# Forward attention: exponentials over three PSUM banks in two slots, and a new TensorE order for it

## The chip, the cores and the metric

The kernel runs on one core of a Trainium2 chip. The metric is the device time of one execution in microseconds. Before the change its median over three runs is 2441.95 us (2440.43 to 2444.49). The engines are TensorE (PE in the profile; PEld is its weight load), VectorE (DVE), ScalarE (ACT), GpSimd (POOL) and SyncE (SP, which here only issues DMAs).

## The reference

One transformer block (2048 tokens, width 512, 32 heads of 16, a dense layer of 1792 with a squared ReLU, modulated layer norms) is computed forward, and then the gradients of all of its inputs but one. What the change touches is the softmax of the forward attention:

```
scores = jnp.einsum('bhqd,bhkd->bhqk', q, k) * Dh ** (-0.5)
p = _softmax(scores, axis=-1)
o = jnp.einsum('bhqk,bhkd->bhqd', p, v)
```

With 32 heads and 2048 x 2048 scores for each, 134 million exponentials have to be taken forward (and once more in the gradient, which the change leaves alone).

## The kernel before

After a short preparation the forward attention runs as 512 *units* (`funits`, NF = 512): 4 chunks of 512 queries, by 8 groups of 4 heads, by 16 tiles of 128 keys. One unit is one key tile of one head group for one query chunk: four heads, each a 128 x 512 block of scores, so four PSUM banks.

For a unit, `fscore` (L611) makes four score products. Each contracts over 32 rows (16 of the head, and one that carries a bound that is subtracted before the exponential), and the four heads use the four row groups of the TensorE array. They go in pairs: two products fill a two-bank tile `psST`, and one ACTIVATE (L622) takes the exponential of both banks, 128 x 1024, into the SBUF tile `ET`. `psST` has three slots (`bufs=3`, L1226), six of the eight PSUM banks.

`fpv` (L624) multiplies a unit's exponentials with the values: four products side by side in four column groups, added into `oacc`, one bank, over the 16 key tiles of a head group. After the 16th, VectorE copies `oacc` out (`ostage`, L640) before the next group may begin; the first unit of a group is called `begins` in the loop, and its `fpv` stands later in the order for that reason.

The eighth bank is `pm` (`mm()`, L157, a pool with one slot). It serves everything else that TensorE does meanwhile: the projections of the later heads in the first quarter, and then, for every query chunk that is finished, the dense layer forward and backward and the weight gradients. This work is cut into steps, one for a unit (`step`, `next_chain`, `next_ds`, and a table `plan` for the first 128 units). Most steps are one product of four matmuls into `pm` that VectorE then copies out (dsT L330, part L255, rz L458 and others); some products are spread over four units (L484, L538) and are read out only after the last. A unit without such a step gets two small filler matmuls (`steady`, L665). Which step belongs to which unit is counted in units, not in time.

The order of the instructions on every engine is the order in which the Python code makes them. TensorE takes them strictly in that order. For unit u it is: the scores of u; the value product of u - 2 (after the step, where that begins a head group); the step; filler. TensorE waits in three kinds of places: a score product waits until the exponential that last read its slot is done, a step waits until VectorE has emptied `pm`, and a value product waits for its exponentials.

Of the kernel before, what the change touches and what calls it, by code (L numbers as in the profile page):

```python
# [14 lines left out]
AF = mybir.ActivationFunctionType  # L15
ALU = mybir.AluOpType
AX = mybir.AxisListType
BF = dt.bfloat16
F32 = dt.float32

P = 128
# [7 lines left out]
SCALE = 0.25  # L29
# [5 lines left out]
def kernel(  # L35
# [8 lines left out]
    TT = n // P  # L44
# [8 lines left out]
    PE = nc.tensor  # L53
    DVE = nc.vector
    ACT = nc.scalar
# [89 lines left out]
    with ExitStack() as ph:  # L145
# [4 lines left out]
        ework = att.enter_context(tc.tile_pool(name="phCe", bufs=4, reuse_waits="tile"))  # L150
        b2row = ffw.tile([1, D], BF, name="b2row")
        racc = ffw.tile([P, 5, D], F32, name="racc")
        pools = {}
# [3 lines left out]
        def mm():  # L157
            products[0] += 1
            return pools["mm"].tile([P, 512], F32, name="pm", tag="pm")
# [21 lines left out]
        def later(lag, f, *args):  # L181
            due.append((unit[0] + lag, f, args, True))
# [4 lines left out]
        def run_due(everything=False):  # L187
            i = 0
            while i < len(due):
                if due[i][0] <= unit[0] or (everything and due[i][3]):  # L190
                    _, f, args, _ = due.pop(i)
                    f(*args)
                else:
                    i += 1
# [400 lines left out]
        funits = [(qc, hg, kt) for qc in range(QC) for hg in range(HG) for kt in range(TT)]  # L595
        fh, fe, fcur, fdone, dense = {}, {}, {}, [], []
# [4 lines left out]
        def fload(qc, hg):  # L601
            i = hg % 2
            kt_sb, qt_sb = kts[i], qts[i]
            rows = list(row_loads(kt_sb, qkT_st[1], hg, slice(0, n)))
            rows += row_loads(qt_sb, qkT_st[0], hg, slice(512 * qc, 512 * qc + 512), m_st)
            for i, (to, fro) in enumerate(rows):
                later(i // (2 if qc == 0 else 1), row_load, to, fro)
            run_due()
            fh[qc, hg] = (qt_sb, kt_sb)

        def fscore(u):  # L611
            qc, hg, kt = funits[u]
            qt_sb, kt_sb = fh[qc, hg]
            ET = ework.tile([P, 4, 512], BF, name="ET", tag="ET")
            fe[u] = ET
            for pair in range(2):
                ps = pools["s"].tile([P, 2, 512], F32, name="psST", tag="psST")
                for hi in range(2):
                    r = 32 * (2 * pair + hi)
                    PE.matmul(ps[:, hi, :], kt_sb[r:r + 32, kt * P:(kt + 1) * P], qt_sb[r:r + 32, :],  # L620
                              start=True, stop=True, tile_position=(r, 0))
                ACT.activation(ET[:, 2 * pair:2 * pair + 2, :], ps[:], AF.Exp, scale=SCALE)  # L622

        def fpv(u):  # L624
            qc, hg, kt = funits[u]
            if kt == 0:
                fcur["o"] = pools["o"].tile([P, 512], F32, name="oacc", tag="oacc")
                if hg == 0:
                    fcur["rr"] = ework.tile([H, 512], F32, name="rrows", tag="rrows", bufs=1)
                    fcur["ou"] = ework.tile([P, 4, HG, P], BF, name="O_un", tag="O_un", bufs=1)  # L630
            oacc = fcur["o"]
            ET = fe.pop(u)
            for hq in range(4):
                h = hg * 4 + hq
                lhsT = vaug[:, kt].rearrange("p h c -> p (h c)")[:, h * (DH + 1):h * (DH + 1) + 32]
                PE.matmul(oacc[32 * hq:32 * hq + 32, :], lhsT, ET[:, hq, :],  # L636
                          start=(kt == 0), stop=(kt == TT - 1), tile_position=(0, 32 * hq), skip_group_check=True)
            if kt == TT - 1:
                ostage = ework.tile([P, 512], F32, name="ostage", tag="ostage", bufs=1)
                DVE.tensor_copy(ostage[:], oacc[:])  # L640
                obf = ework.tile([P, 512], BF, name="obf", tag="obf", bufs=2)
                if u == NF - 1:
                    fcur["last"] = ostage
                    return
                if hg == HG - 1:
                    DVE.tensor_copy(obf[:], ostage[:])
                else:
                    POOL.tensor_copy(obf[:], ostage[:])
                for hq in range(4):
                    h = hg * 4 + hq  # L650
                    later(2, sp, fcur["rr"][h:h + 1, :], ostage[32 * hq + 16:32 * hq + 17, :])
                later(3, sp, fcur["ou"][:, :, hg, :], obf[:], True)
                if hg == HG - 1:
                    fdone.append((u + 7, qc, fcur["rr"], fcur["ou"]))

        def steady(u):
            if 0 <= u < NF and funits[u][2] == TT - 1:
                if dense or dwq or plan:
                    return
                pz = mm()  # L660
                for _ in range(2):
                    PE.matmul(pz[:], ones_bf[:], identb.unsqueeze(1).to_broadcast([P, 4, P]), start=True, stop=True)
            elif 0 <= u < NF:
                for _ in range(2):
                    PE.matmul(fcur["o"][0:DH, :], zeros[:], identb.unsqueeze(1).to_broadcast([P, 4, P]), start=False, stop=False,  # L665
                              tile_position=(0, 0), skip_group_check=True)
# [503 lines left out]
        NF = len(funits)  # L1170
# [44 lines left out]
        def early(u):  # L1215
            return u >= NF - 7 and "L" in loads and "O" not in loads["L"]
# [6 lines left out]
        plan_tasks()  # L1223
        stages = [*range(4, 14), *range(4), None, None, *range(14, 25)]
        with ExitStack() as ph2:
            pools["s"] = ph2.enter_context(tc.tile_pool(name="psS", bufs=3, space=bass.MemoryType.PSUM, reuse_waits="tile"))  # L1226
            pools["o"] = ph2.enter_context(tc.tile_pool(name="psO", bufs=1, space=bass.MemoryType.PSUM, reuse_waits="tile"))
            pools["mm"] = ph2.enter_context(tc.tile_pool(name="psM", bufs=1, space=bass.MemoryType.PSUM, reuse_waits="tile"))
            with tc.manual_schedule(engines={PE.engine, ACT.engine, DVE.engine, SP.engine, POOL.engine}):
                fh[0, 0] = (qts[0], kts[0])  # L1230
                for u in range(NF + 2):
                    unit[0] = u
                    run_due()
                    if u < NF:
                        if funits[u][2] == (10 if u < 7 * TT else 2) and u + TT < NF:
                            fload(*funits[u + TT][0:2])
                        fscore(u)
                    begins = TT <= u - 2 < NF and funits[u - 2][2] == 0
                    if 2 <= u and not begins:
                        fpv(u - 2)  # L1240
                    if u % 4 == 2 and u // 4 < len(stages) and stages[u // 4] is not None:
                        later_stage(stages[u // 4])
                    if u % 4 == 0 and 18 <= u // 4 < 32:
                        turn_weights(u // 4 - 18)
                    count, begun_group = products[0], open_group[0]
                    for f, args in plan.pop(u, ()):
                        f(*args)
                    if not dense and fqueue and fdone and u - 2 >= fdone[0][0]:
                        fqueue.pop(0)
                        qc, rr, ou = fdone.pop(0)[1:]  # L1250
                        ffinish(qc, rr, ou, chunk_loads(qc))
                    elif u < NF - 4 and not early(u):
                        step(u)
                    elif dwq and u >= NF - 2:
                        next_chain()
                    if begins:
                        fpv(u - 2)
                    if u in post:
                        post.pop(u)()
                    if products[0] == count and not (begun_group or open_group[0]):  # L1260
                        steady(u - 2)
                    if early(u):
                        early_finish()
                    if u == NF:
                        tiny = wk.tile([P, 1], F32, name="tiny", tag="tiny", bufs=1)
                        ACT.activation(tiny[:], onesf[:, 0:1], AF.Sqrt)
                while dense:
                    unit[0] += 1
                    run_due()
                    step(unit[0])  # L1270
# [381 lines left out]
    with ExitStack() as ph:  # L1652
        ework = ph.enter_context(tc.tile_pool(name="phIe", bufs=4, reuse_waits="tile"))
# [197 lines left out]
        if True:  # L1851
# [4 lines left out]
            for b in range(NU // 4):  # L1856
                toks, bank = order_t if on_pe(b - 1) else order_n
                for tok in toks:
                    c, i = tok[0], int(tok[1:] or 0)
# [409 lines left out]
```

## Time and profile before

| | |
|---|---|
| median of three runs | 2441.95 us |
| the profiled execution, and its span | 2435.86 us, 2434.1 us |
| first exponential of the forward attention starts, last ends | 37.1 us, 976.7 us |
| busy from 37.1 to 976.7 (939.6 us) | ACT 939.33, PE 872.11, DVE 485.68, POOL 303.62 us |
| the rest of the kernel after that (backward attention and the last gradients) | some 1457 us |

In a row of the costliest groups stand line, engine, operation, what is written and read, the shapes, the count, then the busy time in us and the mean ns of one, then the time that the engine stood idle just before them and what ended it. In a timeline row stand the start and the length in us, the engine and the line, and in brackets idle time before it. A mean of ACT's instructions is longer than their spacing, because an ACTIVATE is recorded from its dispatch, and the next one is dispatched before the one ahead is done.

### The profile page before, as it was taken

How to read it: one execution, taken by the hardware profiler on the slowest of the kernel's cores; microseconds unless marked ns; L12 is line 12 of the kernel's file. 1: busy time of each engine (PE TensorE's matmuls, PEld its weight loads, DVE VectorE, ACT ScalarE, POOL GpSimd, SP SyncE). 2: the span in 40 equal slices, each digit the busy share in tenths (PEclk: the TensorE clock that was granted, in tenths of full speed). 3: DMA queues.
4: the chain of work that ended last, by engine and by line, in shares of the span. 5: the costliest groups of instructions: out<-in, count | busy, mean ns of one | idle time of the engine just before them, and what ended most of it. 6: DMA issues, size and time to landing. Idle time of an engine off the chain costs nothing.

```text
span 2434.1 us, 49843 instructions
## 1 busy us (share of the span) xinstructions
PE 2305.9 (95%) x18929; PEld 770.3 (32%) x19004; DVE 1841.2 (76%) x2443; ACT 2294.7 (94%) x3579; POOL 505.9 (21%) x692
## 2 busy tenths in 40 slices
PE   8999899999999999899999999999999999999999
PEld 3232233333333323432222333222223322223244
DVE  6655374456445645679999999999989999999976
ACT  8999999999999999639999999999999999999965
POOL 2211224213642452220111101111011010110112
PEclk9999999999999999999999999999999999999999
DMA  4578445546674747869999999999999999999997
GB/s 153 137 165 190 111 105 127 137 108 110 120 158 80 139 79 165 213 199 209 205 205 199 209 206 204 202 211 199 207 204 202 210 208 199 203 210 206 207 217 195
DMA packets 1196773, 426.67 MB, mean 175 GB/s; under 512 B 1080407, under 2 KB 1173205, under 8 KB 1196405
## 3 DMA queue, kind: packets, MB, share of 16 engines
q1 hardware_dynamic: 1151524, 364.82, 80.0%
q0 software_dynamic: 23984, 35.35, 8.6%
q10 hardware_dynamic: 21024, 23.32, 3.8%
q8 instruction: 149, 2.44, 0.4%
q14 instruction: 92, 0.75, 0.1%
HBM read 85.46 MB, written 68.95 MB: 63 GB/s over the span
## 4 chain that ended last, share of the span: by engine, by line
ACT 41%; PE 39%; issue 8%; DVE 6%; DMA 4%; ACTq 1%; POOL 1%; SPq 0%; DVEq 0%; another core or an unknown queue 0%; POOLq 0%
ACT E_u L1731 25%; ACT ET L622 11%; PE psST L620 5%; PE dqacc L1814 4%; PE oacc L636 3%; ACT dsT L1891 3%; PE psS_A L1725 3%; PE pm L237 3%; PE psS_B L1725 2%; PE accVK L1787 2%; DMA dsT<-dS_u 2%; PE pm L455 2%; PE pdh L1915 2%; PE pm L538 2%; PE psS_C L1725 2%
## 5 line engine op out<-in xcount | busy, mean ns | idle before, releaser
L1747 DVE TENSOR_TENSOR dS_u<-psD_u,E_u 128x1024 bf16<-128x1024 f32 x1024 | 1180.4, 1217 | 66.1 <-PE psD_u L1745 35.2
L622 ACT ACTIVATE ET<-psST 128x1024 bf16<-128x1024 f32 x1024 | 939.3, 1332 | 0.3
L1731 ACT ACTIVATE E_u<-psS_A 128x512 bf16<-128x512 f32 x768 | 489.1, 637 | 9.4 <-PE psS_C L1725 6.9
L1731 ACT ACTIVATE E_u<-psS_B 128x512 bf16<-128x512 f32 x768 | 484.3, 631 | 9.9 <-PE psD_u L1745 4.6
L1745 PE MATMUL psD_u<-iv,ido 32*128 32x512 bf16 x2048 | 403.1, 386 | 1.1 <-DVE dS_u L1747 1.1
L620 PE MATMUL psST<-qt_sb,kt_sb 32*128 32x512 bf16 x2048 | 318.8, 382 | 43.0 <-ACT ET L622 38.2
L1731 ACT ACTIVATE E_u<-psS_C 128x512 bf16<-128x512 f32 x512 | 324.7, 634 | 2.6 <-PE psS_B L1725 1.3
L1725 PE MATMUL psS_B<-ik,iq 32*128 32x512 bf16 x768 | 293.6, 382 | 10.3 <-ACT E_u L1731 2.6
L1725 PE MATMUL psS_A<-ik,iq 32*128 32x512 bf16 x768 | 291.3, 379 | 9.4 <-ACT E_u L1731 0.7
L1832 POOL TENSOR_TENSOR dQacc<-dQacc,dqtmp 128x512 f32<-128x512 f32 x64 | 81.3, 1271 | 843.2 <-ACT dqtmp L1827 836.8
L1725 PEld LDWEIGHTS <-iq 32*128 32x128 bf16 x2048 | 125.5, 91 | 312.9 <-issue 298.3
L1787 PE MATMUL accVK<-dS_u,qz 128*32 128x512 bf16 x2048 | 212.3, 389 | 0.2 <-DVE dS_u L1747 0.2
L636 PE MATMUL oacc<-ET,vaug 128*32 128x512 bf16 x2048 | 206.5, 391 | 0.0
L1796 PE MATMUL accVK<-E_u,dOs_tok 128*16 128x512 bf16 x2048 | 201.4, 383 | 0.0
L1725 PE MATMUL psS_C<-ik,iq 32*128 32x512 bf16 x512 | 193.7, 378 | 4.2 <-ACT dQacc L1824 0.2
L620 PEld LDWEIGHTS <-kt_sb 32*128 32x128 bf16 x2048 | 90.7, 91 | 315.4 <-issue 290.7
L1814 PE MATMUL dqacc<-dsT,KS_tok 128*32 128x512 bf16 x2048 | 147.3, 386 | 15.6 <-DMA dsT<-dS_u 2.1
L1745 PEld LDWEIGHTS <-ido 32*128 32x128 bf16 x2048 | 105.4, 91 | 91.5 <-issue 83.9
L1891 ACT ACTIVATE dsT<-ptT 128x1024 bf16<-128x1024 bf16 x126 | 131.1, 1041 | 0.0
L255 DVE COPY part<-pm 128x512 f32<-128x512 f32 (+2 forms) x105 | 64.4, 614 | 66.7 <-PE pm L237 64.2
L1787 PEld LDWEIGHTS <-qz 128*32 128x32 bf16 x2048 | 58.4, 94 | 177.2 <-issue 162.4
L1770 PE MATMUL accVK<-dOs_tok,KS_tok 128*16 128x512 bf16 x325 | 103.7, 382 | 0.0
(440 smaller groups left out, 2646.8 us busy)
## 6 DMA issues: line engine op xcount, KB each, us to landing
p_st<-part POOLq DMA_DIRECT2D x36, 256.0 KB, 4.5
kt_sb<-qkT_st POOLq DMA_DIRECT2D x124, 64.0 KB, 3.6
wA<-in_B_w_dram SPq DMA_DIRECT2D x28, 256.0 KB
w_nat<-in_B_w_dram SPq DMA_DIRECT2D x21, 256.0 KB
w2T<-w2T_st SPq DMA_DIRECT2D x21, 256.0 KB
p_st<-part POOLq DMA_DIRECT2D x27, 192.0 KB, 4.2
p_st<-part SPq DMA_DIRECT2D x18, 256.0 KB
part<-p_st SPq DMA_DIRECT2D x18, 256.0 KB
```

The costliest lines, as they stand in the source:

```text
L620: PE.matmul(ps[:, hi, :], kt_sb[r:r + 32, kt * P:(kt + 1) * P], qt_sb[r:r + 32, :], start=True, stop=True, tile_position=(r, 0))
L622: ACT.activation(ET[:, 2 * pair:2 * pair + 2, :], ps[:], AF.Exp, scale=SCALE)
L636: PE.matmul(oacc[32 * hq:32 * hq + 32, :], lhsT, ET[:, hq, :], start=(kt == 0), stop=(kt == TT - 1), tile_position=(0, 32 * hq), skip_grou ...
L1725: PE.matmul(psS[:], st["q"][r:r + 32, qt * P:(qt + 1) * P], st["k"][r:r + 32, kc * 512:kc * 512 + 512], start=True, stop=True, tile_positi ...
L1731: ACT.activation(bst[u][0][:, hq, :], sst.pop((u, hq))[:], AF.Exp, scale=SCALE)
L1745: PE.matmul(psD[:, hi, :], st["do"][r:r + 32, qt * P:(qt + 1) * P], st["v"][r:r + 32, kc * 512:kc * 512 + 512], start=True, stop=True, til ...
L1747: DVE.tensor_tensor(dS_u[:, 2 * pair:2 * pair + 2, :], psD[:], E_u[:, 2 * pair:2 * pair + 2, :], ALU.mult)
L1770: PE.matmul(cur["vk"][0:DH, :], KS_tok[:, 0, D:QPAD], dOs_tok[:, 0, :], start=False, stop=False, tile_position=(0, 0), skip_group_check=True)
L1787: PE.matmul(cur["vk"][32 * hq:32 * hq + 32, :], hst[hg]["qz"][:, qt, hq, :], bst[u][1][:, hq, :], start=(qt == 0), stop=False, tile_positi ...
L1796: PE.matmul(acc[32 * hq:32 * hq + DH, :], dOs_tok[:, qt, (hg * 4 + hq) * DH:(hg * 4 + hq + 1) * DH], E_u[:, hq, :], start=False, stop=(qt ...
L1814: PE.matmul(acc[32 * hq:32 * hq + 32, :], KS_tok[:, kc * 4 + kt, h * DH:h * DH + 32], tT[:, :, hq * 4 + kt, :], start=(kt == 0), stop=(kt ...
L1891: ACT.activation(dst, pt[:], AF.Identity)
```

## The change

The exponentials are taken three banks at a time. `fscore` no longer takes a unit but a *slot number* i: it fills banks 3i to 3i + 2 of the sequence of all 2048 score blocks, whatever unit they belong to, and makes one ACTIVATE of 128 x 1536 (the last has two banks). `psST` has three banks and two slots, again six banks. `ET` holds three banks in five buffers, not four in four. The value product of a unit finds its four blocks in two `ET` tiles.

Three units are four slots now, so the order of TensorE is written for threes of units. With `part` = u % 3 and `first` = 4 (u // 3), the slots of a three are called S0 to S3 here, W0, W1, W2 are the steps of its units and PV the value products:

- part 0: S0, PV, W0, S1
- part 1: W1, S2, PV (PV ahead of W1 where it ends a head group)
- part 2: PV, S3, W2 (S3 behind W2 where PV begins a head group)

```diff
-        def fscore(u):
-            qc, hg, kt = funits[u]
-            qt_sb, kt_sb = fh[qc, hg]
-            ET = ework.tile([P, 4, 512], BF, name="ET", tag="ET")
-            fe[u] = ET
-            for pair in range(2):
-                ps = pools["s"].tile([P, 2, 512], F32, name="psST", tag="psST")
-                for hi in range(2):
-                    r = 32 * (2 * pair + hi)
-                    PE.matmul(ps[:, hi, :], kt_sb[r:r + 32, kt * P:(kt + 1) * P], qt_sb[r:r + 32, :],
-                              start=True, stop=True, tile_position=(r, 0))
-                ACT.activation(ET[:, 2 * pair:2 * pair + 2, :], ps[:], AF.Exp, scale=SCALE)
+        def fscore(i):
+            w = min(3, 4 * NF - 3 * i)
+            if w <= 0:
+                return
+            ET = ework.tile([P, 3, 512], BF, name="ET", tag="ET", bufs=5)
+            ps = pools["s"].tile([P, 3, 512], F32, name="psST", tag="psST")
+            for k in range(w):
+                u, hq = divmod(3 * i + k, 4)
+                qc, hg, kt = funits[u]
+                qt_sb, kt_sb = fh[qc, hg]
+                r = 32 * hq
+                PE.matmul(ps[:, k, :], kt_sb[r:r + 32, kt * P:(kt + 1) * P], qt_sb[r:r + 32, :],
+                          start=True, stop=True, tile_position=(r, 0))
+                fe[u, hq] = ET[:, k, :]
+            ACT.activation(ET[:, 0:w, :], ps[:, 0:w, :], AF.Exp, scale=SCALE)
...
-                PE.matmul(oacc[32 * hq:32 * hq + 32, :], lhsT, ET[:, hq, :],
+                PE.matmul(oacc[32 * hq:32 * hq + 32, :], lhsT, fe.pop((u, hq)),
...
-            pools["s"] = ph2.enter_context(tc.tile_pool(name="psS", bufs=3, space=bass.MemoryType.PSUM, reuse_waits="tile"))
+            pools["s"] = ph2.enter_context(tc.tile_pool(name="psS", bufs=2, space=bass.MemoryType.PSUM, reuse_waits="tile"))
...
-                        fscore(u)
+                    part, first = u % 3, 4 * (u // 3)
                     begins = TT <= u - 2 < NF and funits[u - 2][2] == 0
-                    if 2 <= u and not begins:
+                    ends = u < 2 or funits[u - 2][2] == TT - 1
+                    if part == 0:
+                        fscore(first)
+                    ahead_pv = 2 <= u and not begins and (part != 1 or ends)
+                    if ahead_pv:
                         fpv(u - 2)
+                    if part == 2 and not begins:
+                        fscore(first + 3)
...
-                    if begins:
+                    if part == 1:
+                        fscore(first + 2)
+                    elif part == 2 and begins:
+                        fscore(first + 3)
+                    if 2 <= u and not ahead_pv:
                         fpv(u - 2)
...
+                    if part == 0:
+                        fscore(first + 1)
```

## The prediction

> **What bounds the kernel now.** I read the costliest groups first, then the busy time of each engine by stretches, then timelines of single units. The groups, page and by-shape view:
>
> ```profile
> L622 ACT ACTIVATE ET<-psST 128x1024 bf16<-128x1024 f32 x1024 | 939.3, 1332 | 0.3
> L620 PE MATMUL psST<-qt_sb,kt_sb 32*128 32x512 bf16 x2048 | 318.8, 382 | 43.0 <-ACT ET L622 38.2
> L330 DVE CAST dsT<-pm 128x512 bf16<-128x512 f32 x56 | 38.7, 691 | 84.3 <-PE pm L328 84.3
> L255 DVE COPY part<-pm 128x384 f32<-128x384 f32 x40 | 22.1, 554 | 32.3 <-PE pm L237 31.3 <-DMA w2T<-w2T_st 0.9
> ```
>
> The 1024 exponentials keep ACT busy for 939.3 us with 0.3 us idle: in the forward attention ACT is the bound, one per 917 ns (939.3/1024). TensorE waits for it 38.2 us only. By stretches (length, then PE, PEld, DVE, ACT, POOL):
>
> ```profile
> 37.10:976.70 939.60, 872.11 (x6012) 290.32 (x6072) 485.68 (x987) 939.33 (x1026) 303.62 (x486) 1.00 0.60 129
> ```
>
> TensorE stands at 93%: whether it keeps ACT fed after the change is the question. How long a row takes alone, minimum/median/maximum, from the views of the tiles ET and E_u:
>
> ```profile
> L622 ACT ACTIVATE ET<-psST x1024: 1017/1336/2052, 37.1 to 975.2; 128x1024 bf16<-128x1024 f32 x171
> L1731 ACT ACTIVATE E_u<-psS_A x768: 591/641/718, 1084.9 to 2328.4; 128x512 bf16<-128x512 f32 x192
> ```
>
> And TensorE's timeline where it is tightest, a product (L328) in every unit:
>
> ```profile
> 508.55 1.04 PE L328 MATMUL pm<-gfT,w2T 128*128 128x512 bf16 x4
> 509.52 0.60 PE L620 MATMUL psST<-qt_sb,kt_sb 32*128 32x512 bf16 x4
> 510.53 1.02 PE L328 MATMUL pm<-gfT,w2T 128*128 128x512 bf16 x4 [0.41 <-DVE dsT L330]
> ...
> 513.44 0.40 PE L620 MATMUL psST<-qt_sb,kt_sb 32*128 32x512 bf16 x4
> 513.76 0.40 PE L636 MATMUL oacc<-ET,vaug 128*32 128x512 bf16 x4
> 514.29 1.02 PE L328 MATMUL pm<-gfT,w2T 128*128 128x512 bf16 x4
> 515.25 0.39 PE L620 MATMUL psST<-qt_sb,kt_sb 32*128 32x512 bf16 x4
> 515.57 0.40 PE L636 MATMUL oacc<-ET,vaug 128*32 128x512 bf16 x4
> 516.10 1.02 PE L328 MATMUL pm<-gfT,w2T 128*128 128x512 bf16 x4
> ```
>
> Start to start: scores to value product 0.32 us, value product to step 0.33 (508.22 to 508.55), step to next scores 0.97, and, where VectorE must first empty `pm`, step to next step 1.81 (514.29 to 516.10; VectorE's copy there runs from 515.35 for 0.69). Four score matmuls that find their slots free run side by side, 0.39 us for all.
>
> **The exponentials.** One more bank costs 1017 - 591 = 426 ns, so a three-bank one at ACT's full rate takes 917 + 427 = 1344 ns. Bounds: nothing of the fixed part saved, 1.5 x 917 = 1376; the fixed part saved whole is what 1344 says already. I take 1344, since the two solo rows give the slope directly. 682 x 1.344 + 0.917 = 917.5 us against 939.4: **-21.9 us** if ACT stays fed.
>
> **How much lateness ACT bears.** With ACT idle, a score product at 452.93 let ACT start at 453.42: 0.49 us. A waiting engine resumes some 0.05 us after its release (VectorE done 516.04, TensorE 516.10). Slot i + 2 may start 0.05 after exponential i ends; for ACT to go on without a gap it must start by 2 x 1.344 - 0.49 - (1.017 + 0.427) = 0.75 after it. So scores may be 0.70 us late. Before, with three slots, it was 2 x 0.917 + 0.917 - 0.49 - 1.017 - 0.05 = 1.19 us.
>
> **Where lateness comes from.** Call it L for each slot; from one S to the next it grows by their distance on TensorE less 1.344.
> - S3: the value product ahead of it needs the exponential of S1, the very one that frees S3's slot. So S3 begins one value product after the release: L = 0.32 whatever came before. This resets the account once in three units.
> - S3, W2, S0: 0.32 + 0.97 = 1.29. L = 0.27.
> - S0, PV, W0, S1: by TensorE alone 0.32 + 0.33 + 0.97 = 1.62. But W0 can't start before VectorE has emptied `pm` of W2, 1.81 after W2's start, so S0 to S1 is 1.81 as well: L = 0.27 + 0.47 = 0.74, a gap of 0.03.
> - S1, W1, S2: nothing but scores lies between W0 and W1 now. TensorE alone: 1.29. With the wait on `pm` 1.81: L = 0.70 + 0.47 = 1.17, **a gap of 0.47 us on ACT**. Behind the waiting step stand S2 and two value products; ACT, and nobody else, pays.
> - S2, PV, PV, S3: 0.32 x 3 and a wait; reset.
>
> So a three with a new 512-wide product in each unit loses 0.50 us, twice its gain (22 us/171 = 0.13). With a 384-wide product (copy 0.55, step to step 1.46, step to scores 0.76, from 403.65 and 404.41) all distances shrink: in three of them L ends at 0.3, no gap. Inside a product that is spread over units there is no `pm` wait: L ends at 0.5, no gap. Filler waits for nothing.
>
> **Counting.** I put every unit's step in its place by the order of the trace. Of the 171 threes, 37 have new 512-wide products (or as slow) in W2, W0 and W1: 37 x 0.50 = 18.5 us. 14 have wide, narrow, wide: L = 0.27 + 0.26 + 0.33 = 0.86, a gap of 0.16: 2.2. Ten others have wide W0 and W1: some 0.15 each, 1.5. The 12 ends of L538 hold `pm` for two VectorE operations (0.69 + 0.68), 2.30 us to the next step (view below); 9 of them fall in W2 or W0, where the next step follows soon: 2.30 - 0.55 + 0.75 = 2.50 between slots, L = 0.13 + 1.16, gap 0.59: 5.0. The rest, no gap.
>
> ```profile
> 431.15 0.61 PE L538 MATMUL pm<-w_nat,sT 128*128 128x512 bf16 x2
> 431.69 0.38 PE L543 MATMUL pm<-b2row,ones_bf 1*128 1x512 bf16 x1
> 431.70 1.02 PE L620 MATMUL psST<-qt_sb,kt_sb 32*128 32x512 bf16 x4
> 432.65 0.40 PE L636 MATMUL oacc<-ET,vaug 128*32 128x512 bf16 x4
> 433.45 0.81 PE L237 MATMUL pm<-tk,h_c 128*128 128x384 bf16 x4 [0.40 <-DVE ftmp L548]
> ```
>
> **The small parts.** TensorE issues the same matmuls; the scores' own time falls where pairs had run one after another (0.21 each), and that is in the distances above. Scores are made up to a unit sooner at a head group's start: at units 16 and 32 the last row of `qt_sb` lands 0.5 and 0.3 us ahead of its use now, so some 0.5 each is lost: 1 us; all other loads land 4 us ahead or more. No DMA is moved on SP's or POOL's queue. The five `ET` buffers cost nothing: the value products that free one stand ahead, in TensorE's order, of the scores that need it; without that cover ACT would wait one value product, 0.4. VectorE's work is unchanged, but products come in closer pairs, so a copy may stand behind L461's 0.68 us; I set 0, with 0 to +10 for the range.
>
> Sum: -21.9 + 18.5 + 2.2 + 1.5 + 5.0 + 1.0 = **+6.3 us**. The profiled execution took 2435.86 us (span 2434.1 and 1.8 around it), 0.25% under the median; set on the median, 2441.95 + 6.3 = **2448 us**. 0.2%, 4.9 us, is about what a measurement of this kernel tells from no change.
>
> The gaps sit beside the row [0.41 <-DVE dsT L330]: with one unit between two products TensorE already waits. The Trainium skill, Perfetto Trace Analysis, Optimizing Tensor Performance, says that independent matmul groups should rotate through different PSUM banks, so that one's evacuation overlaps the next one's matmuls; the change goes against it twice, two slots for three, and two `pm` groups nearly back to back. Taken as a rule for every such neighbour it makes the third rival's sum; by the rows only the wide ones count.
>
> **Rivals.**
> 1. *ACT stays fed* (faster). It decides how soon `pm` is free: were step to step 1.70 us and not 1.81, L in a wide three would be 0.27 + 0.36 + 0.36 = 0.99, a gap of 0.29 and not 0.50, and at 1.50 none. Then 2442 - 22 = 2420, with half the gaps 2434. For it: TensorE waits for ACT now, 38.2 us; the gaps are differences of 0.1 us. Against: 1.81 is a measured spacing with VectorE idle before the copy.
> 2. *The change doesn't do what it says*: three banks cost 1376. Then nothing is gained, and the gaps shrink by some 0.1 in a wide three (lateness grows by 0.03 less a slot), to about 23 us; 2442 + 23 = 2465. Against: the two solo rows.
> 3. *Every new pair in W0 and W1 makes a gap*, since VectorE's other work (486 us in the stretch) gets in the way of copies it now meets closer together. 102 threes have new products in both, wide or narrow: 102 x 0.5 + 1 = 52, so 2442 - 22 + 52 = 2472. For it: L461 follows each of the 42 products of L458 with 0.68 us. Against: a copy now starts 0.04 us after its matmul nearly always.
>
> **The numbers.** Forecast (2438 to 2458) 0.53; ACT fed, all or by half (below 2438) 0.18; rival 2 0.03; rival 3, wholly or in part (above 2458) 0.26. Of the forecast's 0.53, 0.24 lies under 2446.8, which is 0.2% above the median: faster 0.18, same 0.24, slower 0.29 + 0.03 + 0.26 = 0.58. Range: 2430 (a third of my gaps) to 2474 (rival 3), which leaves some 0.12 below it, where ACT is fed nearly throughout, and 0.08 above. The forecast's own: 2438 to 2458.
>
> **What would show it.** ACT ET x683, spacing 1.34 us where it is fed; its stretch some 946 us and not 939.6; ACT's idle time before ET from 0.3 to near 28 us, ended by psST; idle before steps on DVE up to several times what it is (13 us in all in the list of waits); a timeline of L328's units with W0, S1 and a long wait before W1. Wrong would be: gaps before slots other than S2, a third of the idle time or less (rival 1), a spacing of 1.37 (rival 2), or gaps in threes of narrow products (rival 3).

## The result, and the profile after

The changed kernel takes 2452.29 us, median of six runs (2448.81 to 2457.53), against 2441.80 for the kernel before (six runs, 2439.04 to 2444.49): a ratio of 1.0044, 95% interval 1.0032 to 1.0057. It is 10.5 us slower, where 6.3 were forecast.

The groups, page of the changed kernel (line, engine, operation, tiles, shapes, count, busy us, mean ns, idle time just before and what ended it):

```profile
L625 ACT ACTIVATE ET<-psST 128x1536 bf16<-128x1536 f32 (+1 forms) x683 | 926.9, 1499 | 24.1 <-PE psST L622 23.1
...
L622 PE MATMUL psST<-qt_sb,kt_sb 32*128 32x512 bf16 x2048 | 270.4, 385 | 37.9 <-ACT ET L625 33.9
```

Before, ACT waited 0.3 us in the whole forward attention. Now it waits 24.1, for scores. TensorE's score time fell from 318.8 to 270.4 us, as three products for one slot run side by side, where before a pair was often alone. Its wait for ACT stayed near where it was (33.9 against 38.2 us), so now each of the two engines waits for the other in turn.

The stretch from the first to the last exponential, before and then after (length, then PE, PEld, DVE, ACT, POOL busy, granted clock, DMA):

```profile
37.10:976.70 939.60, 872.11 (x6012) 290.32 (x6072) 485.68 (x987) 939.33 (x1026) 303.62 (x486) 1.00 0.60 129
976.70:2434.00 1457.30, 1403.69 (x12729) 465.90 (x12738) 1327.54 (x1374) 1329.82 (x2514) 191.53 (x174) 0.99 1.15 206
```

```profile
37.10:988.10 951.00, 834.26 (x6011) 267.91 (x6072) 486.39 (x987) 926.86 (x684) 304.60 (x486) 1.00 0.59 127
988.10:2450.00 1461.90, 1405.04 (x12729) 465.96 (x12738) 1327.91 (x1374) 1330.37 (x2515) 191.30 (x174) 0.99 1.15 205
```

The stage, as this stretch is called from here on, grew from 939.6 to 951.0 us, so by 11.4 us: the whole of the difference of the medians. The 4.5 us by which the stretch behind it is longer lie in work that the change does not touch (see the last section).

From the record of each exponential, end to end: where ACT is fed, the spacing is 1343 ns. Spacings above that add up to 34.0 us in 108 places: 26.7 us in 68 of them ahead of S2, 5.9 us in 34 ahead of S1, 1.4 us ahead of S3 and S0. ACT without them would have taken 917.0 us. (The row above shows 24.1 and not 34.0 of it: it counts idle time up to the start of a record, and the first exponential, which met an idle ACT, is on record for 1.45 us, 0.11 more than the spacing.)

One three of units with a product in each, TensorE's timeline (start, length, line, what is written and read, count, idle time before it):

```profile
517.08 0.39 PE L622 MATMUL psST<-qt_sb,kt_sb 32*128 32x512 bf16 x3
517.40 1.04 PE L328 MATMUL pm<-gfT,w2T 128*128 128x512 bf16 x4
518.37 0.39 PE L622 MATMUL psST<-qt_sb,kt_sb 32*128 32x512 bf16 x3
518.69 0.40 PE L638 MATMUL oacc<-ET,vaug 128*32 128x512 bf16 x4
519.22 1.02 PE L328 MATMUL pm<-gfT,w2T 128*128 128x512 bf16 x4
520.17 0.39 PE L622 MATMUL psST<-qt_sb,kt_sb 32*128 32x512 bf16 x3
521.02 1.02 PE L328 MATMUL pm<-gfT,w2T 128*128 128x512 bf16 x4 [0.46 <-DVE dsT L330]
521.98 0.39 PE L622 MATMUL psST<-qt_sb,kt_sb 32*128 32x512 bf16 x3
522.30 0.62 PE L638 MATMUL oacc<-ET,vaug 128*32 128x512 bf16 x8
```

And ACT's timeline over the same time:

```profile
518.05 4.13 ACT L625 ACTIVATE ET<-psST 128x1536 bf16<-128x1536 f32 x3
522.48 2.79 ACT L625 ACTIVATE ET<-psST 128x1536 bf16<-128x1536 f32 x2 [0.29 <-PE psST L622]
```

S3 is at 517.08, W2 at 517.40, S0 at 518.37, W0 at 519.22 (1.82 after W2), S1 at 520.17, W1 at 521.02 (1.80 after W0, and 0.46 of it is plain waiting for VectorE), S2 at 521.98, 1.81 after S1. ACT has taken three exponentials without a gap; the fourth, for S2, comes late. S3 follows after the two value products, and the account is reset.

### The profile page after: what moved, and what is told of

Its sections match the earlier page's. It is cut to its first block, busy times and chain, and to the rows that moved or that the text cites. A ratio compares the mean times of both kernels' runs of the same rounds, so it can differ in the third digit from the quotient of the medians.

```text
span 2450.0 us, 49663 instructions
## 1 busy us (share of the span) xinstructions
PE 2269.4 (93%) x18927; PEld 747.8 (31%) x19004; DVE 1842.3 (75%) x2443; ACT 2282.8 (93%) x3238; POOL 506.7 (21%) x692
## 4 chain that ended last, share of the span: by engine, by line
ACT 41%; PE 33%; issue 10%; DVE 8%; DMA 5%; ACTq 1%; SPq 0%; DVEq 0%
ACT E_u L1745 23%; ACT ET L625 13%; PE dqacc L1828 4%; DMA dsT<-dS_u 3%; PE psST L622 3%; ACT dsT L1905 3%; PE psS_A L1739 2%; PE oacc L638 2%; PE psS_B L1739 2%; PE accVK L1801 2%; PE pm L237 2%; PE pm L455 2%; PE psS_C L1739 2%; ACT dqtmp L1841 1%; PE pdh L1929 1%
## 5 line engine op out<-in xcount | busy, mean ns | idle before, releaser
L625 ACT ACTIVATE ET<-psST 128x1536 bf16<-128x1536 f32 (+1 forms) x683 | 926.9, 1499 | 24.1 <-PE psST L622 23.1
L622 PE MATMUL psST<-qt_sb,kt_sb 32*128 32x512 bf16 x2048 | 270.4, 385 | 37.9 <-ACT ET L625 33.9
L638 PE MATMUL oacc<-ET,vaug 128*32 128x512 bf16 x2048 | 218.7, 389 | 6.9 <-ACT ET L625 6.2
L622 PEld LDWEIGHTS <-kt_sb 32*128 32x128 bf16 x2048 | 74.3, 91 | 336.5 <-issue 329.2
L255 DVE COPY part<-pm 128x512 f32<-128x512 f32 (+2 forms) x105 | 64.5, 615 | 74.4 <-PE pm L237 71.5
```

What stands on the lines that cost most here:

```text
L622: PE.matmul(ps[:, k, :], kt_sb[r:r + 32, kt * P:(kt + 1) * P], qt_sb[r:r + 32, :], start=True, stop=True, tile_position=(r, 0))
L625: ACT.activation(ET[:, 0:w, :], ps[:, 0:w, :], AF.Exp, scale=SCALE)
L638: PE.matmul(oacc[32 * hq:32 * hq + 32, :], lhsT, fe.pop((u, hq)), start=(kt == 0), stop=(kt == TT - 1), tile_position=(0, 32 * hq), skip_g ...
```

## The experiments

### W1 behind S2: only the order

```diff
-                    ends = u < 2 or funits[u - 2][2] == TT - 1
...
-                    ahead_pv = 2 <= u and not begins and (part != 1 or ends)
+                    ahead_pv = 2 <= u and not begins
                     if ahead_pv:
                         fpv(u - 2)
-                    if part == 2 and not begins:
-                        fscore(first + 3)
+                    if part > 0:
+                        fscore(first + 1 + part)
...
-                    if part == 1:
-                        fscore(first + 2)
-                    elif part == 2 and begins:
-                        fscore(first + 3)
```

> Only TensorE's order differs from the changed kernel: part 1 is PV, S2, W1 (was W1, S2, PV), part 2 is PV, S3, W2 in all cases. If the gaps come from W1 standing right behind W0 while VectorE still holds pm (my account), a wide three loses 0.18 us and not 0.50, the stage from the first to the last exponential goes from 951.0 to 932 to 936 us, and the kernel to 2434 to 2438, below both kernels. If VectorE's load is the cause, the stage stays near 951, because VectorE's work is the same. If it is the value product that waits in front of S3, it also stays near 951, because that one stands where it was.

Measured: stage 940.4 us; kernel 2441.53 us (ten runs) against 2441.12 for the kernel before on the same chip (13 runs), ratio 0.9998, interval 0.9981 to 1.0014. So this order alone takes back the change's whole loss, and no more. The exponentials' row on the page of this kernel:

```profile
L625 ACT ACTIVATE ET<-psST 128x1536 bf16<-128x1536 f32 (+1 forms) x683 | 925.6, 1508 | 14.8 <-PE psST L622 11.4
```

End to end, the gaps fell from 34.0 to 23.4 us; those ahead of S2 went from 26.7 to 0.1, and those ahead of S1 rose from 5.9 to 20.8. The order thus decides where the gaps are: now W1, W2 and W0 follow one another with the wait on pm, and S1 behind them pays. VectorE's work and the value product in front of S3 were left as they were, so neither alone made the gaps ahead of S2. The stage is 4 us longer than the range I had given, and so is the kernel; 3.8 us of the gaps lie in three stretches where TensorE's clock was halved (last section), which I had left out of every expectation.

### A short hold of pm

```diff
-                DVE.tensor_copy(G["ds"][:, fc, :], pds[:])
+                DVE.tensor_copy(G["ds"][:, fc, 0:P], pds[:, 0:P])
+                rest_of(G["ds"][:, fc, :])
```

The other five lines are changed in the same way; `rest_of` writes columns 128 and up with a scalar_tensor_tensor from the first 128.

> The changed kernel, but in the dense layer's steps (L255, L330, L389, L458, L545, L548) VectorE reads only the first 128 columns of pm, and fills the other columns from SBUF with those 128 at about the same cost in VectorE time. Left out: the values of columns 128 and up in these products. pm is free some 0.5 us sooner, VectorE is as busy as before. If pm's hold makes the gaps, ACT's idle time before ET falls from 24 us to under 8 and the stage from 951.0 to 923 to 929 us. If VectorE's load makes them, the stage stays at 948 to 953.

The exponentials' row on the page of this kernel:

```profile
L637 ACT ACTIVATE ET<-psST 128x1536 bf16<-128x1536 f32 (+1 forms) x683 | 923.4, 1526 | 14.1 <-PE psST L634 12.8
```

Measured: stage 937.5 us, gaps 20.5 (14.1 in the row above, where under 8 were expected). The range of 923 to 929 was missed, but the stage moved by 13.5 of the 22 to 28 us that the hold of pm should give, and VectorE was busier than before (533.7 us in the stage, not 486.4), so its load by itself can't be what made the gaps that went. Of the gaps that are left, 6.5 us lie in five stretches at half clock, and 5.5 in the first 128 units, whose projections were not shortened.

### S3 ahead of the value product

```diff
-                    if ahead_pv:
-                        fpv(u - 2)
                     if part == 2 and not begins:
                         fscore(first + 3)
+                    if ahead_pv:
+                        fpv(u - 2)
```

> The changed kernel with S3 ahead of the value product in part 2. If the lateness of 0.32 us that this product gives S3 were the cause, every wide three would lose 0.32 less and the stage would fall to some 936 us. By my account nothing is won: the product then lies between S3 and S0, so S0 is as late as before, and the gap before S2 stays 0.5 us: stage 949 to 954 us.

Measured: stage 956.2 us; gaps ahead of S2 27.7, ahead of S1 10.3. Nothing is won, as expected; the stage is 2 us above my range. The 0.32 us in front of S3 were no cause, because the product only moved to the other side.

### The order of the change undone

```diff
                     if part == 0:
                         fscore(first)
-                    ahead_pv = 2 <= u and not begins and (part != 1 or ends)
+                    fscore(first + 1 + part)
+                    ahead_pv = 2 <= u and not begins
                     if ahead_pv:
                         fpv(u - 2)
-                    if part == 2 and not begins:
-                        fscore(first + 3)
...
-                    if part == 1:
-                        fscore(first + 2)
-                    elif part == 2 and begins:
-                        fscore(first + 3)
...
-                    if part == 0:
-                        fscore(first + 1)
```

> The changed kernel without its order: S0 and S1 at the start of part 0, S2 and S3 at the start of parts 1 and 2, each part then PV and W. If any order with two slots loses as much (TensorE's load, or two slots as such), the stage stays near 951 or is longer. By my account the distance between two steps is what counts; here S and PV lie between any two, so the stage is shorter than with the order of the change, 943 to 949 us, though not as short as with W1 behind S2.

Measured: stage 954.6 us, gaps 37.7, 30.0 of them ahead of S0. My range of 943 to 949 was wrong: the plain order is 3.6 us longer than that of the change, not shorter. The expectation went by the distance between two steps alone and left out the account of lateness, which gives these gaps. S2, S3 and S0 each follow the slot ahead of them by a value product and a step, up to 1.81 us, and only S1 comes close behind S0. From S1 to S0 the lateness so grows three times by up to 0.47, to 1.4 against the 0.70 that ACT bears: a loss of up to 0.7 in a wide three, ahead of S3 and S0. There the gaps are, 6.9 us in 35 places ahead of S3 and 30.0 in 88 ahead of S0; this sum was made after the run. Compared with the first experiment (940.4) it still says that the number of slots does not fix the loss: the order alone moves the stage by 14 us.

### Controls: the short hold in the kernel before, and two slots there

The first control has the edits of the short hold in the kernel before.

> The kernel before, with the short reads of pm of the second experiment (columns 128 and up of the dense layer's products are left out and filled from SBUF). With three slots TensorE may be 1.19 us late and is not, so a pm that is free 0.5 us sooner gains nothing: stage 938 to 941 us, as before (939.6). If the short reads speed the kernel up in another way than by closing the gaps of two slots, the stage falls here too.

Measured: stage 940.4 us, gaps 1.6. With three slots pm's hold costs nothing.

```diff
-            pools["s"] = ph2.enter_context(tc.tile_pool(name="psS", bufs=3, space=bass.MemoryType.PSUM, reuse_waits="tile"))
+            pools["s"] = ph2.enter_context(tc.tile_pool(name="psS", bufs=2, space=bass.MemoryType.PSUM, reuse_waits="tile"))
```

> The kernel before with two slots of two banks for three, so the number of slots alone (two banks of PSUM lie idle). Bearable lateness falls from 1.19 to 2 x 0.917 - 0.49 - 1.017 - 0.05 = 0.28 us, while a unit's value product and wide step put the next scores 1.62 - 0.92 = 0.70 behind the release: a gap of 0.42 us in each unit with a wide product. Stage 1010 to 1040 us. If slots are not what bears the lateness, it stays near 940.

Measured: stage 1040.8 us, within 1 us of the upper end. The groups of this kernel in the stage:

```profile
L622 ACT ACTIVATE ET<-psST 128x1024 bf16<-128x1024 f32 x1024 | 970.7, 1029 | 70.1 <-PE psST L620 61.4 <-ACT ET L622 0.9
```

The mean of an ACTIVATE fell from 1332 to 1029 ns, near the 1017 of one that meets an idle engine: with a bearable lateness of 0.28 us, most exponentials start with no time to spare, and 322 of the 1024 come late, by 0.32 us on average. The third slot was worth 101 us to the kernel before (12.9 us of the gaps lie around eight stretches at half clock). The wider exponential gave part of it back, as a slot then lasts 1.34 us.

### Hold or load

Twice the same reads of pm, and as much VectorE work behind them without pm:

```diff
                 DVE.tensor_copy(G["ds"][:, fc, :], pds[:])
+                DVE.tensor_copy(G["ds"][:, fc, :], pds[:])
```

```diff
                 DVE.tensor_copy(G["ds"][:, fc, :], pds[:])
+                once_more(G["ds"][:, fc, :])
```

Both edits stand at L255, L330, L389 and L458; `once_more` is a scalar_tensor_tensor of the copied tile with ones, in place.

> The changed kernel; VectorE reads pm twice (the same copy again) in L255, L330, L389 and L458, so pm is held 0.69 us longer. By my account step to step becomes 2.50 us, which alone is 7.5 us for a wide three against 5.4 of ACT: stage 1035 to 1065 us. If the hold of pm were not the cause, the stage would grow no more than in the next run, which gives VectorE as much work.

> The changed kernel; behind each of the same four reads VectorE gets one more operation of about 0.69 us on SBUF (times one, in place), so its load is that of the run above, but pm is free as early as in the changed kernel, except where the next copy stands behind the extra operation (after L458, whose own operations and this one take 2.5 us). By my account most gaps stay as they are: stage 951 to 975 us. If VectorE's load makes the gaps, 1035 to 1065 as above.

The exponentials' rows on the two pages, the longer hold first:

```profile
L629 ACT ACTIVATE ET<-psST 128x1536 bf16<-128x1536 f32 (+1 forms) x683 | 936.6, 1486 | 137.6 <-PE psST L626 135.9
L634 ACT ACTIVATE ET<-psST 128x1536 bf16<-128x1536 f32 (+1 forms) x683 | 929.7, 1496 | 47.9 <-PE psST L631 45.1
```

Measured: stage 1074.1 us with the longer hold, 977.6 with as much more work (VectorE is busy for 625 and 629 us of the stage) and pm free in time. Both lie a little above their ranges (by 9 and 3 us). The longer hold makes the stage grow by 123 us, the work without it by 27. Not all of the 96.5 us between is the hold by itself: there are 19 and 6 stretches at half clock in the two stages, and 54 and 14 us of the gaps lie around them. Gaps elsewhere grew from 31 us in the changed kernel to 103 and 47. So by either count the hold costs several times what the load does. The 27 are not nothing: the waits of TensorE in the run with more work show steps waiting for copies that stood behind the extra operation:

```profile
PE pm L463 <- DVE part L260: 11.5, 21, 1.1
PE pm L463 <- DVE rz L466: 9.1, 15, 1.1
...
PE pm L334 <- DVE dsT L336: 7.1, 13, 1.0
```

(Engine and line waited for, us in all, times, longest; L463 here is L455 before.) In these waits VectorE's load acts by way of the hold: a copy that starts late holds pm as long as one that takes long.

### Both causes taken away, and an order chosen for each three

The first of these has the order of the first experiment and the short hold together.

> Order of the first experiment and the short reads of pm of the second together (columns 128 and up of the dense layer's products are left out and filled from SBUF). If the neighbourhood of W0 and W1 and the hold of pm are all that stands between the change and its gain, the stage comes to 920 to 928 us, near the 917.5 of ACT alone, a stretch at half clock adding 1 to 2 each. If something else makes gaps, it stays above 932.

The exponentials' row on the page of this kernel:

```profile
L637 ACT ACTIVATE ET<-psST 128x1536 bf16<-128x1536 f32 (+1 forms) x683 | 920.8, 1555 | 7.0 <-PE psST L634 5.8
```

Measured: stage 927.8 us, gaps 10.7, at the upper edge of the range, with no stretch at half clock in the stage. Of the 23.4 us of gaps with that order 12.7 are gone; up to 3.8 of these lay around stretches at half clock and may not be the hold's. 3.5 of the 10.7 that remain lie in the first 128 units, whose products are not shortened. What the other 7 are was not taken apart.

The second chooses among eight orders, three by three, from a table worked out by the account of lateness. The edit puts the tokens of the chosen order around the step of each unit:

```diff
+        def run_order(u, after):
+            g = u // 3
+            for token in ORDERS[int(CHOICE[g])][u % 3][after].split():
+                if token[0] == "S":
+                    fscore(4 * g + int(token[1]))
+                elif 2 <= 3 * g + int(token[1]) < NF + 2:
+                    fpv(3 * g + int(token[1]) - 2)
```

> The changed kernel with one of eight orders for each three of units, chosen by the account of lateness (which steps of the three hold pm, and for how long) so that the gaps on ACT add up to least: by that account 8.5 us in all, where W1 behind S2 throughout has 15.5 (19.6 measured, apart from the stretches at half clock). If the account is right, stage 930 to 937 us and kernel 2431 to 2438, under the kernel before. If order can't do more than W1 behind S2 did, the stage is 938 us or longer and the kernel equals the one before.

Measured: stage 935.0 us, 4.6 below the kernel before; gaps 17.9, of which 4.1 in five stretches at half clock. The other 13.8 are more than the 8.5 of the account. The groups of this kernel in the stage:

```profile
L625 ACT ACTIVATE ET<-psST 128x1536 bf16<-128x1536 f32 x682 | 922.9, 1513 | 11.2 <-PE psST L622 9.1
```

ACT's wait for scores is 9.1 us, against 23.1 with the order of the change. The kernel takes 2438.6 us (12 runs), just above the range of 2431 to 2438, against 2440.8 (17 runs) for the kernel before: ratio 0.9989, interval 0.9975 to 1.0003. The stage is shorter in the profile; in the whole time the gain is not told from none. So the idea of the change can be carried out without loss, but with one bank for pm the best of these orders brings at most some 5 of its 22 us.

## Why the prediction was right

The time lies in the range and the sign was right; the loss came out two thirds larger than forecast (10.5 us for 6.3, and 11.4 in the stage). Each step of the account can be held against the trace.

- *The exponential at 1344 ns.* Measured 1343, and 917.0 us for ACT without gaps against 917.5. The rival in which three banks cost 1376 is gone.
- *Lateness that ACT bears, and S3's reset.* Gaps stand ahead of S2 and S1, and nearly none ahead of S3 and S0 (1.4 of 34.0 us), as the four distances had it. The 5.9 us ahead of S1 are more than the 0.03 of a wide three; part of them are ends of L538 in W2.
- *The wait on pm.* W0 to W1 takes 1.80 us in the timeline shown, 1.81 in the sum. TensorE's waits for VectorE in the stage add up to 61 us; 13.8 before.
- *A wide three loses 0.50.* The 37 threes of this kind lost 16.8 us, 0.45 each, where 18.5 were forecast.
- *Wide, narrow, wide: 2.2 forecast.* The 14 lost 3.4, 0.24 each and not 0.16.
- *Ten others with wide W0 and W1: 1.5 forecast.* They lost 2.4 us.
- *The ends of L538: 5.0 forecast (nine times 0.59 is 5.3).* The threes with the end of such a group lost about 6.5 us, one of them 1.3, since the halved clock fell on it.
- *The rest: 1.0 forecast, for two head groups.* It lost some 5 us in small amounts, but not there: the threes with units 16 and 32 show no gap, so the term was not seen.

So the step that came out short is the counting. The gaps measured 34.0 us, not the 28.2 of the sum (1.0 of it for the head groups). By the list, the wide threes lost 1.7 us less than forecast, the three kinds after them 3.6 more, and the threes that I had set at none some 4 more; up to 3.2 us of all this lie around two stretches at half clock, which the sum did not know. The mechanism and its size in the common case were right. One comparison in the text was not: the 0.50 us of a wide three is nearly four times the gain of 0.13, not twice. With the gain at 22.6 us, 34.0 - 22.6 = 11.4 us is the growth of the stage.

The third rival (every pair of products makes a gap) is answered by the same counts: threes of narrow products lost 0.1 us in seven. The first rival, that ACT stays fed, failed on its own point: step to step was 1.80 us and not 1.70.

With pm's turnaround cut short and W1 moved, 23.3 of the 34.0 us of gaps are gone; without those around stretches at half clock it is 20 of 31. So the experiments show the hold of pm and the neighbourhood of two steps as the cause of most of the loss. They fit the rule of the Trainium skill (Perfetto Trace Analysis, Optimizing Tensor Performance) that independent matmul groups should rotate through different PSUM banks. A second bank for pm could not be tried with this change, since scores, oacc and pm take all eight. What the rule does not say is when one bank is enough: with three score slots it was (939.6 us with the long hold, 940.4 with the short one).

## What to carry to other kernels

A wider instruction that saves a fixed cost on the bounding engine also takes a buffer away where the memory is full, so the saving (here 126 ns in three units) has to be set against the lateness that the other engine may still have (here 0.70 us for 1.19). Add up, for each buffer, the distance from one fill to the next on the engine that fills it, with its waits, and compare it with the bounding engine's period; where one step's result has to be emptied before the next step starts, put other work between the two. A wait that costs nothing under a deep queue is the first thing to look at when the queue gets shorter.

## What the runs showed that I had not expected

TensorE's clock is granted at half for stretches of 3.4 us, or of 6.8 to 13.7, and two slots pay for them where three mostly do not. In the kernel before, by stretches (columns as above; the granted clock stands third from the end):

```profile
738.00:758.00 20.00, 18.25 (x136) 6.53 (x133) 8.58 (x14) 20.00 (x23) 6.72 (x13) 1.00 0.49 101
758.00:761.00 3.00, 3.00 (x16) 0.59 (x11) 2.28 (x4) 3.00 (x5) 0.46 (x1) 0.50 0.25 40
```

And in the changed kernel:

```profile
295.00:314.00 19.00, 14.89 (x112) 5.11 (x113) 14.82 (x43) 18.70 (x15) 5.08 (x10) 1.00 0.21 54
314.00:317.00 3.00, 3.00 (x22) 0.87 (x20) 2.08 (x5) 2.41 (x3) 0.00 (x0) 0.50 0.01 3
```

In the first, TensorE runs at 0.50 from 758 to 761 us and ACT is busy in all 3.00 us; in the second ACT loses 0.6 of 3.0. Around such stretches the changed kernel's gaps come to 1.2 and 2.0 us, the kernel before has none at its one, and its control with the short hold 0.7 us at one of three. The Trainium skill (TensorE: Matmul & The Clock Gate, Part 1) describes a clock that falls to half after an idle window of some 3.4 us. No such window stands ahead of this one: in the 20 us before 758 TensorE was busy for 18.25, and its longest gap was 0.53 us. But it was less busy just before: 2.72 of the last 3.4 us ahead of 758, 1.81 of 3.4 ahead of 314. All twelve profiles show the same. In the 3.4 us ahead of each of their 121 falls, TensorE's busy share has a median of 0.63, and it is under 0.80 ahead of 110 of them. In the 8248 stretches as long with no fall behind them the median is 0.96, but 642 of these are under 0.80 too. So a low share goes ahead of nearly every fall and does not bring one by itself. What does stays open. The waits that a change adds may have a part in it: 19 of these stretches lie in the stage of the kernel with the longest hold. That was not tested.

The rest of the kernel, which none of the edits touches, varies with them too. Time behind the last exponential, and how much of it ran at half clock, from all twelve profiles:

| kernel | time behind the stage, us | of it at half clock, us |
|---|---|---|
| S3 ahead of the value product | 1456.6 | 10.2 |
| before | 1457.4 | 17.2 |
| before, two slots | 1458.8 | 17.6 |
| W1 behind S2, short hold | 1464.8 | 21.7 |
| changed | 1461.9 | 23.9 |
| chosen orders | 1466.3 | 23.9 |
| W1 behind S2 | 1463.3 | 27.3 |
| before, short hold | 1464.3 | 30.7 |
| the order undone | 1466.5 | 32.0 |
| more VectorE work | 1465.4 | 34.1 |
| pm read twice | 1467.7 | 41.0 |
| short hold | 1472.2 | 44.4 |

The 4.5 us by which the changed kernel's profile is longer there lie within the scatter of this table. The time grows with the half clock, but that is not all of it: two kernels with 23.9 us differ by 4.4, and 6.7 us more at half the clock can't hold back more than 3.4 us of work. Where the rest comes from stays open.
